# Transposing q, k and x of a whole block with one DMA each, and loading the ninth chunks of two batches together

## The chip, the cores and the metric

The kernel runs on one core of a Trainium2 chip. The metric is the device time of one execution in microseconds. Engines: TensorE (PE, with its weight loads shown as PEld), VectorE (DVE), ScalarE (ACT), GpSimd (POOL) and SyncE (SP). In this kernel SP does no arithmetic: its queue issues, in program order, all loads and all DMA transposes. POOL's queue issues nearly all stores of the output.

## The reference

Attention within chunks of 64 positions (8 batches, 8 heads, 576 positions, so nine chunks per batch and head, head dimension 64), then a feed-forward layer with squared ReLU over the 4608 tokens:

```python
q_c = q.reshape(B, H, nc, 64, D)          # the same for k and v
scores = np.matmul(q_c, k_c.transpose(0, 1, 2, 4, 3)) / np.sqrt(D)
attn = softmax(scores)                    # over the last axis
x = np.matmul(attn, v_c)                  # -> tokens (B*S, H*D)
h = np.maximum(x @ w_in, 0.0)             # 512 -> 2048
out = h * h @ w_out                       # 2048 -> 512
```

Inputs and output are float32; the kernel's matmuls take bf16 operands.

## The kernel before

The tokens are cut into 18 **groups** of 256 (four chunks of one batch), and two groups make a **block** (`blocks`), nine in all, numbered 0 to 8. Eight chunks of a batch fill two groups; the ninth chunks of all batches are collected in groups 14 and 15 (`rest`), which form block 7. `is_whole(g)` is false for these two alone. Within a group `t` (0, 1) is the 128-token tile and `p` the half of 64 partitions in it.

A group passes through these steps, whose names are the keys of the plan further down:
- loads (`qk_pieces`, `v_pieces`): q in one DMA for a whole group, k in two (one per `t`), V in even heads (`v_even`) and odd heads (`v_odd`, whose chunks sit on the opposite half of the partitions). For a group of ninth chunks every chunk has its own DMA: four of q, four of k, eight of V. The list from `runs(g)` says which stretches belong together.
- `C` (`cast_qk`): q and k are cast to bf16 into `qkb`, by POOL for groups below 8 and by ScalarE from there on.
- `TD` (`transpose_qk_dma`): one DMA transpose from `qkb` to `qkT` (16 tiles of 128 by 128), from group 4 on. Earlier groups are transposed by TensorE.
- `SC` (`scores`): 32 small matmuls of `qkT` into PSUM and one exponential on ScalarE into `e`.
- `AV` (`values`): 32 small matmuls of `e` with V, and the division by the sums on VectorE into `x`.
- `XT` (`transpose_x`): x is transposed into the block's `xT`, by one DMA per group from group 6 on (8 tiles).

Then the block goes through the layer: `ffn_in` (16 hidden tiles, four 512-column matmuls each, ReLU on ScalarE, square on VectorE or ScalarE into `gT`), and `ffn_out` (seven products of a Strassen-like scheme with 16 matmuls each; block 0 uses a plain form).

The order is written by hand. The program runs block after block; each yield of `ffn_in` and `ffn_out` is a **slot** (16 of the hidden layer, or 32 in block 1, then 14 of the output). `plan` says which step of another block is put in after which slot: while block j runs its layer, attention of block j+1 (`nxt`) is done (SC, AV, XT), and block j+2 (`far`) is loaded, cast and transposed (C, TD). One load is issued per slot of `go_slots`. For j from 3 on C stands at slots 18 and 22 and TD at 20 and 24; in j = 2 two slots later or so, in j = 1 at 36, 40 and 42, 45. The schedule is manual: each engine executes its instructions in this order[...].

Buffers: `qk` input tiles 5, `qkb` 2, `qkT` 4, `e` 3, `x` 3 groups, `xT` 2 blocks.

Of the kernel before, what the change touches and what calls it, by code (L numbers as in the profile page):

```python
# [10 lines left out]
FP32 = mybir.dt.float32  # L11
BF16 = mybir.dt.bfloat16
# [5 lines left out]
def kernel(  # L18
# [22 lines left out]
    blocks = [[g, g + 1] for g in range(0, n_grp, 2)]  # L41


    CH = GT // 4
    n_ch = S // CH
    whole = [[(b, CH * (4 * i + c)) for c in range(4)] for b in range(B) for i in range(2)]
    rest = [[(b, CH * (n_ch - 1)) for b in range(b0, b0 + 4)] for b0 in range(0, B, 4)]
    chunks = whole[:-2] + rest + whole[-2:]

    def is_whole(g):  # L50
# [27 lines left out]
    NV = 5  # L78
    NO = 2 * NV + 1
    v_even = [w_pool.tile([128, 2, n_hp, D + 1], FP32, name=f"ve_sb{i}") for i in range(NV)]  # L80
    v_odd = [w_pool.tile([128, n_hp, D + 1], FP32, name=f"vo_sb{i}") for i in range(NO)]
    for vt in v_even:
        nc.gpsimd.memset(vt[:, :, :, D:D + 1], 1.0)
    for vt in v_odd:
        nc.gpsimd.memset(vt[:, :, D:D + 1], 1.0)

    qk = {}

    def runs(g):

        for t in range(2):
            (b, s), (b1, s1) = chunks[g][2 * t:2 * t + 2]
            if b == b1:
                yield t, 0, 2 * CH, b, s
            else:
                yield t, 0, CH, b, s
                yield t, CH, CH, b1, s1

    def qk_pieces(g):
        q_sb = in_pool.tile([128, 2, H, D], FP32, name="q_sb")  # L100
        k_sb = in_pool.tile([128, 2, H, D], FP32, name="k_sb")
        qk[g] = (q_sb, k_sb)

        def pairs(dst, src, p, m, b, s):
            return lambda: nc.sync.dma_start(
                out=dst.rearrange("p t h d -> p (t h d)")[p:p + m // 2, :].rearrange(
                    "p (h e) -> p h e", h=H),
                in_=src[b, :, s:s + m, :].rearrange("h (s i) d -> s h (i d)", i=2))

# [8 lines left out]
        for t, p, m, b, s in runs(g):  # L118
            yield lambda t=t, p=p, m=m, b=b, s=s: nc.sync.dma_start(
                out=k_sb[p:p + m, t, :, :],  # L120
                in_=k[b, :, s:s + m, :].rearrange("h s d -> s h d"))

# [4 lines left out]
    for g in range(n_grp):  # L127
        if is_whole(g):
            if g % 2 == 0:
                first = n_odd  # L130
                n_odd += 5
            b, s = chunks[g][0]
            for c in range(4):
                odd_tile[g, c] = first + g % 2 * 2 + (c + 1) // 2
            odd_loads[g] = [(first, CH, CH, b, s), (first + 1, 0, 2 * CH, b, s + CH),
                            (first + 2, 0, 2 * CH, b, s + 3 * CH)] if g % 2 == 0 else [
                                (first + 3, 0, 2 * CH, b, s + CH), (first + 4, 0, CH, b, s + 3 * CH)]
        else:
            for c in range(4):
                odd_tile[g, c] = n_odd + c // 2  # L140
            odd_loads[g] = [(n_odd + c // 2, (1 - c % 2) * CH, CH, b, s)
                            for c, (b, s) in enumerate(chunks[g])]
            n_odd += 2

    def v_pieces(g):
        for t, p, m, b, s in runs(g):
            yield lambda t=t, p=p, m=m, b=b, s=s: nc.sync.dma_start(
                out=v_even[g % NV][p:p + m, t, :, 0:D],
                in_=v[b, 0::2, s:s + m, :].rearrange("h s d -> s h d"))
        for n, p, m, b, s in odd_loads[g]:  # L150
            yield lambda n=n, p=p, m=m, b=b, s=s: nc.sync.dma_start(
                out=v_odd[n % NO][p:p + m, :, 0:D],
                in_=v[b, 1::2, s:s + m, :].rearrange("h s d -> s h d"))

    def go(pieces):
# [55 lines left out]

    def transpose_qk(g, q_pool, k_pool):
        if ("qkT", g) not in state:
            state["qkT", g] = att_pool.tile(
                [128, 2, 2, n_hp, 128], BF16, name="qkT", bufs=4)
        qkT = state["qkT", g]
        for which, pool in enumerate((q_pool, k_pool)):
            if pool is None:
                continue
            copy = nc.scalar.copy if which else nc.vector.tensor_copy  # L220
            if pool is ps_ffn:
                bank = pool.tile([128, 512], FP32, name="ps_ffn")
            else:
                bank = pool.tile([128, 1024], FP32, name="ps_att")
            bank = bank.bitcast(BF16)[:, 0:1024]
            transpose_paired(g, which, bank)
            copy_paired(copy, qkT[:, which], bank)
# [22 lines left out]
                rhs=ident[:, None, :].to_broadcast([128, m, 128]), start=True, stop=True)  # L250

    def cast_qk(g):
        qkb = att_pool.tile([128, 2, 2 * H * D], BF16, name="qkb", bufs=2)
        state["qkb", g] = qkb

        copy = nc.gpsimd.tensor_copy if g < 8 else nc.scalar.copy
        q_sb, k_sb = (x.rearrange("p t h d -> p (t h d)") for x in qk[g])
        copy(
            out=qkb[:, 0].rearrange("p (i h d) -> p i h d", i=2, h=H),
            in_=q_sb.rearrange("p (h i d) -> p i h d", h=H, i=2))  # L260
        copy(out=qkb[:, 1], in_=k_sb)

    def transpose_qk_dma(g):
        qkb = state.pop(("qkb", g))
        qkT = att_pool.tile([128, 2, 2, n_hp, 128], BF16, name="qkT", bufs=4)
        state["qkT", g] = qkT
        nc.sync.dma_start_transpose(
            out=qkT.rearrange("c w t h q -> c (w t h) q"),
            in_=qkb.rearrange("p w c -> p (w c)"))

    def scores(g):
        qkT = state.pop(("qkT", g))
# [10 lines left out]
        for hp in range(n_hp):  # L283
            for t in range(2):
                for a in range(2):
                    for p in range(2):
# [5 lines left out]
                            lhsT=qkT[64 * a:64 * a + 64, 1, t, hp, cols],  # L292
                            rhs=queries(a, t, hp, p),
                            start=True, stop=True)
        e = att_pool.tile([128, 2, n_hp, 2, 64], BF16, name="e")
        state["e", g] = e
        e_out, s_in = e.rearrange("p a h t q -> p (a h t q)"), ps
        if by_plane:
# [4 lines left out]
    def values(g, tiles=(0, 1)):  # L303
        e = state["e", g]
        veb = v_even[g % NV].bitcast(BF16)
        vob = [v_odd[odd_tile[g, c] % NO].bitcast(BF16) for c in range(4)]
        if 0 in tiles:
            state["x", g] = att_pool.tile([128, 2, n_hp, 2, D], BF16, name="x", bufs=3)
# [22 lines left out]
    def transpose_x(g):  # L331
# [16 lines left out]
        copy = nc.vector.tensor_copy if g == blocks[1][0] else nc.scalar.copy  # L348
        copy(out=dst, in_=psb)

    C, TD = cast_qk, transpose_qk_dma
    SC, AV, XT = scores, values, transpose_x

    def TA(g):
# [58 lines left out]
    def ffn_out(j):  # L413
# [50 lines left out]
        def store(dma, o_sb, half, col, t):  # L464
            g = blocks[j][half]
            b, s0 = chunks[g][0]
            t0 = b * S + s0
            if not is_whole(g):

                for p in range(2):  # L470
                    dma.dma_start(
                        out=out.rearrange("(b s) d -> s b d", s=S)[
                            s0:s0 + CH, b + p:b + 4:2, col:col + HD],
                        in_=o_sb[p * CH:(p + 1) * CH].rearrange("p (t d) -> p t d", d=HD))
# [135 lines left out]
    for j, grps in enumerate(blocks):  # L610
# [15 lines left out]
        elif j == 1:  # L626
# [7 lines left out]
                    at(slot, f, g)  # L634
            for i, g in enumerate(far):
                at(36 + 4 * i, C, g)
                at(42 + 3 * i, TD, g)
            at(2, sum_quarters(b11_p_b12, b11, b12), None)
            at(12, sum_quarters(b12_p_b22, b12, b22), None)
            at(20, sum_quarters(b21_p_b22, b21, b22), None)  # L640
            phases = [ffn_in(1, [(0, 256, FT_ORDER), (256, 256, FT_ORDER)]), ffn_out(1)]
        else:
            loads, go_slots = pieces(far), range(32)
            slots = {SC: (6, 6), AV: (9, 13), XT: (12, 16), C: (18, 22), TD: (20, 24)}
            if j == 3:
                slots.update({SC: (8, 8), AV: (10, 14), XT: (13, 17)})
                go_slots = [*range(6), *range(13, 32)]
# [15 lines left out]
        slot = 0  # L663
        for phase in phases:
# [40 lines left out]
```

## Time and profile before

| what | value |
|---|---|
| median of 3 runs | 288.24 us (284.66 to 289.51) |
| profiled execution: time, span | 286.88 us, 285.1 us |
| TensorE busy | 270.0 us (95%) |
| VectorE, ScalarE, POOL busy | 186.4, 163.3, 57.6 us |
| SP's DMA queue (q1) | 137744 packets, 47.33 MB, 76.2% of 16 engines |
| DMA transposes of q,k | 14, median 6.6 us from issue to landing |
| DMA transposes of x | 12, median 3.4 us |
| k loads of 128 KB, V loads of 64 KB (ninth chunks among them) | 8 at 3.9 us; 8 even at 3.5 and 24 odd at 3.9 us |

"Busy" counts the time in which an engine executes; in TensorE's case the ends of pipelined matmuls are modelled. The granted TensorE clock was 1.00 all through. The list of DMA issues gives for each kind the median time from issue to landing, waiting behind other transfers included. Times in the timeline count from the start of the span.

### The profile page before, as it was taken

What the parts mean: (1) busy time and instruction counts of PE and PEld (TensorE: products, weight loads), DVE (VectorE), ACT (ScalarE), POOL (GpSimd) and SP (SyncE); (2) the same over time, 40 slices, a digit from 0 to 9 for tenths busy, and PEclk for the clock granted to TensorE, in tenths of its full rate; (3) what the DMA queues carried; (4) which work ended last, traced back from release to release, by engine and by line L of the source; (5) the groups of instructions that cost most, each with busy time, mean ns of one, the idle gap of its engine ahead of it and who ended that gap; (6) DMA issues with size and microseconds to landing.
All of it is one profiled execution on the core that took longest, in us unless ns stands there. A gap on an engine that the chain in (4) does not pass through costs nothing. (4 is left out here: it accounts for less than half of the span.)

```text
span 285.1 us, 7166 instructions
## 1 busy us (share of the span) xinstructions
PE 270.0 (95%) x2951; PEld 175.5 (62%) x2954; DVE 186.4 (65%) x303; ACT 163.3 (57%) x277; POOL 57.6 (20%) x92
## 2 busy tenths in 40 slices
PE   2999999999999999999999999999799989999994
PEld 1554454788774587458645864586358734874583
DVE  1254614898943695589549954995389538965792
ACT  1557705786358762966396639663866287218710
POOL 2028935153171004000300030003000400050012
PEclk9999999999999999999999999999999999999999
DMA  7999999999999999999999899599999962132003
GB/s 204 236 298 322 380 351 223 328 225 213 213 232 259 229 215 247 261 233 170 256 219 215 176 260 245 107 134 196 212 221 184 257 113 39 37 96 55 1 24 125
DMA packets 140817, 57.10 MB, mean 200 GB/s; under 512 B 110640, under 2 KB 137520, under 8 KB 140784
## 3 DMA queue, kind: packets, MB, share of 16 engines
q1 hardware_dynamic: 137744, 47.33, 76.2%
q0 software_dynamic: 2896, 9.18, 9.7%
q8 instruction: 23, 0.38, 0.6%
q10 hardware_dynamic: 144, 0.13, 0.1%
q14 instruction: 10, 0.08, 0.1%
HBM read 36.70 MB, written 9.44 MB: 162 GB/s over the span
## 5 line engine op out<-in xcount | busy, mean ns | idle before, releaser
L380 PE MATMUL ps_ffn<-xT,w_in_bf 128*128 128x512 bf16 (+1 forms) x648 | 130.5, 356 | 0.9 <-POOL w_in_bf L169 0.3
L395 DVE TENSOR_TENSOR gT<-rl 128x512 bf16<-128x512 f32 (+2 forms) x130 | 73.6, 593 | 65.4 <-ACT rl L391 63.6
L391 ACT ACTIVATE rl<-ps_ffn 128x512 f32<-128x512 f32 (+2 forms) x162 | 86.0, 548 | 27.3 <-PE ps_ffn L380 24.4
L380 PEld LDWEIGHTS <-w_in_bf 128*128 128x128 bf16 x648 | 61.2, 98 | 58.0 <-POOL w_in_bf L169 1.0
L448 PEld LDWEIGHTS <-w_st 128*128 128x128 bf16 x640 | 61.7, 98 | 8.8 <-DVE w_st L408 1.4
L408 DVE TENSOR_TENSOR w_st<-gT 128x2048 bf16<-128x2048 bf16 x40 | 47.3, 1219 | 0.2
L448 PE MATMUL ps_ffn<-w_out_bf,w_st 128*128 128x256 bf16 x384 | 45.1, 273 | 0.3
L476 POOL DMA_DIRECT2D out_dram<-o_sb x25 | 17.8, 714 | 128.3 <-DVE o_sb L408 123.7
L448 PE MATMUL ps_ffn<-w_sum,w_st 128*128 128x256 bf16 x256 | 29.6, 273 | 0.0
L448 PEld LDWEIGHTS <-gT 128*128 128x128 bf16 x256 | 24.7, 98 | 4.6 <-DVE gT L395 0.3
L325 DVE TENSOR_TENSOR x<-ps_att,rec 128x512 bf16<-128x512 f32 x36 | 24.9, 691 | 1.2
L528 ACT COPY o_sb<-ps_ffn 128x512 f32<-128x512 f32 (+1 forms) x8 | 4.5, 560 | 35.4 <-PE ps_ffn L448 35.4
L301 ACT ACTIVATE e<-ps_att 128x1024 bf16<-128x1024 f32 x18 | 18.0, 1021 | 6.7 <-PE ps_att L290 6.7
L393 ACT ACTIVATE gT<-rl 128x512 bf16<-128x512 f32 (+2 forms) x32 | 18.4, 576 | 1.0
L448 PE MATMUL ps_ffn<-w_out_bf,gT 128*128 128x256 bf16 x128 | 15.4, 273 | 0.0
L448 PE MATMUL ps_ffn<-w_sum,gT 128*128 128x256 bf16 x128 | 15.3, 273 | 0.0
L538 PE MATMUL ps_ffn<-w_out_bf,gT 128*128 128x512 bf16 x61 | 14.2, 379 | 0.3 <-issue 0.2
L169 POOL CAST w_in_bf<-w_st 128x512 bf16<-128x512 f32 (+2 forms) x12 | 9.6, 816 | 19.2 <-DMA w_st<-in_moe_w_in_dram 18.9
L290 PEld LDWEIGHTS <-qkT 64*64 64x64 bf16 x576 | 6.2, 110 | 9.4 <-issue 3.6
L501 ACT COPY n<-ps_ffn 128x512 f32<-128x512 f32 (+1 forms) x9 | 4.8, 539 | 11.9 <-PE ps_ffn L448 11.9
L290 PE MATMUL ps_att<-qkT 64*64 64x64 bf16 x576 | 8.3, 198 | 3.4 <-DMA qkT<-qkb 3.0
L317 PEld LDWEIGHTS <-e 64*64 64x64 bf16 x576 | 6.5, 107 | 7.4 <-issue 2.2
(53 smaller groups left out, 167.7 us busy)
## 6 DMA issues: line engine op xcount, KB each, us to landing
q_sb<-in_q_dram SPq DMA_DIRECT2D x16, 512.0 KB, 6.4
out_dram<-o_sb POOLq DMA_DIRECT2D x29, 256.0 KB, 4.6
k_sb<-in_k_dram SPq DMA_DIRECT2D x24, 256.0 KB, 5.9
ve_sb<-in_v_dram SPq DMA_DIRECT2D x32, 128.0 KB, 4.2
w_st<-in_moe_w_in_dram SPq DMA_DIRECT2D x8, 512.0 KB, 6.3
w_st<-in_moe_w_out_dram SPq DMA_DIRECT2D x8, 512.0 KB, 5.8
vo_sb<-in_v_dram SPq DMA_DIRECT2D x24, 128.0 KB, 3.8
k_sb<-in_k_dram SPq DMA_DIRECT2D x4, 512.0 KB, 6.7
```

Of the source, the lines that this page charges most:

```text
L169: copy(out=dst, in_=st[:, rows].rearrange("p a (f t) -> p a t f", t=2)[:, :, t])
L290: nc.tensor.matmul(out=ps[64 * c:64 * c + 64, o0:o0 + 64], lhsT=qkT[64 * a:64 * a + 64, 1, t, hp, cols], rhs=queries(a, t, hp, p), start=T ...
L301: nc.scalar.activation(out=e_out, in_=s_in, func=AF.Exp, scale=scale)
L325: nc.vector.tensor_tensor(out=x[:, t].rearrange("p h a d -> p a h d"), in0=o[:, :, :, 0:D], in1=rec.to_broadcast([128, 2, n_hp, D]), op=AL ...
L380: nc.tensor.matmul(out=h[:, 0:n], lhsT=w_in_bf[:, dt, ft * 128:(ft + 1) * 128], rhs=xT[:, c // 128:(c + n) // 128, dt, :], start=(dt == 0) ...
L391: nc.scalar.activation(out=rl[:, 0:n], in_=h[:, 0:n], func=AF.Relu)
L393: nc.scalar.activation(out=gT[:, ft, c:c + n], in_=rl[:, 0:n], func=AF.Square)
L395: nc.vector.tensor_tensor(out=gT[:, ft, c:c + n], in0=rl[:, 0:n], in1=rl[:, 0:n], op=ALU.mult)
L408: engine.tensor_tensor(out=out, in0=in0, in1=in1, op=op)
L448: nc.tensor.matmul(out=outs[t], lhsT=a[:, i, t * 128:(t + 1) * 128], rhs=b[:, i, :], start=(first and i == 0 and (last or t == 0)), stop=( ...
L476: dma.dma_start(out=out[t0:t0 + HT, col:col + HD].rearrange("(t p) d -> p t d", p=128), in_=o_sb.rearrange("p (t d) -> p t d", d=HD))
L538: nc.tensor.matmul(out=o_ps[tt], lhsT=gT[:, ft, tt * 128:(tt + 1) * 128], rhs=w_out_bf[:, ft, :], start=(ft == 0), stop=(ft == n_ft - 1))
```

## The change

Three edits:
1. From group 6 on, q and k of both groups of a block are cast into one `qkb` tile (one buffer of a block in place of two of a group) and transposed by one DMA of 32 tiles (`TDB`), after both casts. `qkT` becomes a block tile with two buffers. Groups 4 and 5 keep a DMA each. C and TDB stand at slots 18, 20 and 22 (j = 2: 20, 22 and 24; j = 1: 36, 40 and 44).
2. The x of both groups of a block is one tile (two buffers), and one DMA of 16 tiles transposes it at the second group's place in the plan. `e` goes from three buffers to two.
3. The ninth chunks are ordered so that batches b and b+1 are the two tiles `t` of a half of the partitions and b+4, b+5 those of the other. k of a half then comes in one DMA (two per group instead of four), V's even and odd heads in two each (four per group instead of eight). `v_odd` becomes one tile with eleven slices, so that two neighbouring slices can be one destination.

```diff
-    rest = [[(b, CH * (n_ch - 1)) for b in range(b0, b0 + 4)] for b0 in range(0, B, 4)]
+    rest = [[(b0 + t + p * (B // 2), CH * (n_ch - 1)) for t in range(2) for p in range(2)]
+            for b0 in range(0, B // 2, 2)]
...
-    v_odd = [w_pool.tile([128, n_hp, D + 1], FP32, name=f"vo_sb{i}") for i in range(NO)]
+    v_odd = w_pool.tile([128, NO, n_hp, D + 1], FP32, name="vo_sb")
...
+        if not is_whole(g):
+            for p in range(2):
+                b, s = chunks[g][p]
+                yield lambda p=p, b=b, s=s: nc.sync.dma_start(
+                    out=k_sb[p * CH:(p + 1) * CH].rearrange("p t h d -> p (t h) d"),
+                    in_=k.rearrange("b h s d -> s (b h) d")[s:s + CH, b * H:(b + 2) * H])
+            return
...
+        if not is_whole(g):
+            n = odd_tile[g, 0] % NO
+            for a, dst in ((0, v_even[g % NV]), (1, v_odd[:, n:n + 2])):
+                for p in range(2):
+                    b, s = chunks[g][p ^ a]
+                    yield lambda a=a, p=p, b=b, s=s, dst=dst: nc.sync.dma_start(
+                        out=dst[p * CH:(p + 1) * CH].rearrange("p t h d -> p (t h) d")[:, :, 0:D],
+                        in_=v.rearrange("b (h a) s d -> a s (b h) d", a=2)[
+                            a, s:s + CH, b * n_hp:(b + 2) * n_hp])
+            return
...
     def cast_qk(g):
-        qkb = att_pool.tile([128, 2, 2 * H * D], BF16, name="qkb", bufs=2)
-        state["qkb", g] = qkb
+        if g % 2 == 0:
+            state["qkb", g // 2] = att_pool.tile(
+                [128, 2, 2, 2 * H * D], BF16, name="qkb", bufs=1)
+        qkb = state["qkb", g // 2][:, g % 2]
...
+    def transpose_qk_dma_block(g):
+
+        for i in range(2):
+            state["qkT", g + i] = qkT_of(g + i)
+        nc.sync.dma_start_transpose(
+            out=state["qkT", "block", g // 2].rearrange("c g w t h q -> c (g w t h) q"),
+            in_=state["qkb", g // 2].rearrange("p g w c -> p (g w c)"))
...
-        e = att_pool.tile([128, 2, n_hp, 2, 64], BF16, name="e")
+        e = att_pool.tile([128, 2, n_hp, 2, 64], BF16, name="e", bufs=2)
...
         if g >= FIRST_DMA_X:
-            nc.sync.dma_start_transpose(out=dst, in_=x.rearrange("p t h a d -> p (t h a d)"))
+
+            if g % 2:
+                nc.sync.dma_start_transpose(
+                    out=xTs[j].rearrange("p t h q -> p (t h) q"),
+                    in_=state["x", "block", g // 2].rearrange("p g t h a d -> p (g t h a d)"))
             return
...
                 at(36 + 4 * i, C, g)
-                at(42 + 3 * i, TD, g)
+            at(44, TDB, far[0])
...
-            slots = {SC: (6, 6), AV: (9, 13), XT: (12, 16), C: (18, 22), TD: (20, 24)}
+            slots = {SC: (6, 6), AV: (9, 13), XT: (12, 16), C: (18, 20), TD: 22}
...
-                slots = {SC: (8, 10), AV: (12, 15), XT: (15, 18), C: (20, 23), TD: (22, 25)}
+                slots = {SC: (8, 10), AV: (12, 15), XT: (15, 18), C: (20, 22), TD: 24}
...
-            for f in (C, TD):
-                for i, g in enumerate(far):
-                    at(slots[f][i], f, g)
+            for i, g in enumerate(far):
+                at(slots[C][i], C, g)
+            if far:
+                at(slots[TD], TDB, far[0])
```

More of the change, by code (lines that the diff above doesn't have):

```diff
@@ L80 @@
     v_even = [w_pool.tile([128, 2, n_hp, D + 1], FP32, name=f"ve_sb{i}") for i in range(NV)]
-    v_odd = [w_pool.tile([128, n_hp, D + 1], FP32, name=f"vo_sb{i}") for i in range(NO)]
+    v_odd = w_pool.tile([128, NO, n_hp, D + 1], FP32, name="vo_sb")
     for vt in v_even:
         nc.gpsimd.memset(vt[:, :, :, D:D + 1], 1.0)
-    for vt in v_odd:
-        nc.gpsimd.memset(vt[:, :, D:D + 1], 1.0)
+    nc.gpsimd.memset(v_odd[:, :, :, D:D + 1], 1.0)
     qk = {}
[L89 to L97, printed above, removed]
     def qk_pieces(g):
@@ L117, in qk_pieces @@
             return
[L118 to L121, printed above, removed]
+        if not is_whole(g):
[5 more added lines that the diff above has]
+            return
+        for t in range(2):
+            b, s = chunks[g][2 * t]
+            yield lambda t=t, b=b, s=s: nc.sync.dma_start(
+                out=k_sb[:, t, :, :],
+                in_=k[b, :, s:s + 2 * CH, :].rearrange("h s d -> s h d"))
     odd_tile, odd_loads = {}, {}
@@ L138 @@
         else:
+            assert n_odd % NO < NO - 1
             for c in range(4):
                 odd_tile[g, c] = n_odd + c // 2
-            odd_loads[g] = [(n_odd + c // 2, (1 - c % 2) * CH, CH, b, s)
-                            for c, (b, s) in enumerate(chunks[g])]
             n_odd += 2
     def v_pieces(g):
[L146 to L149, printed above, removed]
+        if not is_whole(g):
[8 more added lines that the diff above has]
+            return
+        for t in range(2):
+            b, s = chunks[g][2 * t]
+            yield lambda t=t, b=b, s=s: nc.sync.dma_start(
+                out=v_even[g % NV][:, t, :, 0:D],
+                in_=v[b, 0::2, s:s + 2 * CH, :].rearrange("h s d -> s h d"))
         for n, p, m, b, s in odd_loads[g]:
             yield lambda n=n, p=p, m=m, b=b, s=s: nc.sync.dma_start(
-                out=v_odd[n % NO][p:p + m, :, 0:D],
+                out=v_odd[p:p + m, n % NO, :, 0:D],
                 in_=v[b, 1::2, s:s + m, :].rearrange("h s d -> s h d"))
@@ L213, in transpose_qk @@
         if ("qkT", g) not in state:
-            state["qkT", g] = att_pool.tile(
-                [128, 2, 2, n_hp, 128], BF16, name="qkT", bufs=4)
+            state["qkT", g] = qkT_of(g)
         qkT = state["qkT", g]
@@ L261, in cast_qk, with qkT_of @@
         copy(out=qkb[:, 1], in_=k_sb)
+    def qkT_of(g):
+        if g % 2 == 0:
+            state["qkT", "block", g // 2] = att_pool.tile(
+                [128, 2, 2, 2, n_hp, 128], BF16, name="qkT", bufs=2)
+        return state["qkT", "block", g // 2][:, g % 2]
     def transpose_qk_dma(g):
-        qkb = state.pop(("qkb", g))
-        qkT = att_pool.tile([128, 2, 2, n_hp, 128], BF16, name="qkT", bufs=4)
-        state["qkT", g] = qkT
+        state["qkT", g] = qkT = qkT_of(g)
         nc.sync.dma_start_transpose(
             out=qkT.rearrange("c w t h q -> c (w t h) q"),
-            in_=qkb.rearrange("p w c -> p (w c)"))
+            in_=state["qkb", g // 2][:, g % 2].rearrange("p w c -> p (w c)"))
+    def transpose_qk_dma_block(g):
[4 more added lines that the diff above has]
+            in_=state["qkb", g // 2].rearrange("p g w c -> p (g w c)"))
     def scores(g):
@@ L305, in values @@
         veb = v_even[g % NV].bitcast(BF16)
-        vob = [v_odd[odd_tile[g, c] % NO].bitcast(BF16) for c in range(4)]
+        vob = [v_odd[:, odd_tile[g, c] % NO].bitcast(BF16) for c in range(4)]
         if 0 in tiles:
-            state["x", g] = att_pool.tile([128, 2, n_hp, 2, D], BF16, name="x", bufs=3)
+            if g % 2 == 0:
+                state["x", "block", g // 2] = att_pool.tile(
+                    [128, 2, 2, n_hp, 2, D], BF16, name="x", bufs=2)
+            state["x", g] = state["x", "block", g // 2][:, g % 2]
         x = state["x", g]
@@ L349, in transpose_x @@
         copy(out=dst, in_=psb)
-    C, TD = cast_qk, transpose_qk_dma
+    C, TD, TDB = cast_qk, transpose_qk_dma, transpose_qk_dma_block
     SC, AV, XT = scores, values, transpose_x
@@ L472, in store @@
                         out=out.rearrange("(b s) d -> s b d", s=S)[
-                            s0:s0 + CH, b + p:b + 4:2, col:col + HD],
+                            s0:s0 + CH, b + p * (B // 2):b + p * (B // 2) + 2, col:col + HD],
                         in_=o_sb[p * CH:(p + 1) * CH].rearrange("p (t d) -> p t d", d=HD))
```

## The prediction

> **What bounds the kernel now.** I read the page first: busy time by engine, then the chain that ended last, then the list of waits, then the timeline of TensorE (PE) and of SP's queue around each wait.
>
> ```profile
> PE 270.0 (95%) x2951; PEld 175.5 (62%) x2954; DVE 186.4 (65%) x303; ACT 163.3 (57%) x277; POOL 57.6 (20%) x92
> ...
> PE 17%; DMA 4%; DVE 1%; issue 0%
> ```
> ```profile
> PE ps_att L290 <- DMA qkT<-qkb: 3.0, 3, 1.6
> ...
> PE ps_ffn L380 <- DMA xT<-x: 0.2, 1, 0.2
> ```
> TensorE bounds it: 270.0 of 285.1 us. Of the 15.1 us idle, 6.4 lie in the first 20 us (13.62 busy there) and 3.9 in the last 25 (21.14 busy), which the change doesn't touch. What it can remove is the second fence (waits of PE from 20 us on): three waits for transposed q,k and one for transposed x, **3.2 us** or 1.1%. The timeline puts them in block 5 (0.3 at 146.9), block 7 (1.55 at 203.97) and block 8 (1.17 at 232.66, and x 0.22 at 225.78). A change within 2% (5.8 us) can hardly be told from none.
>
> ```profile
> 160.00:180.00 20.00, 20.00 (x220) 12.71 (x218) 12.60 (x20) 12.65 (x20) 2.85 (x4) 1.00 0.98 222
> 180.00:200.00 20.00, 19.90 (x178) 14.25 (x177) 15.81 (x23) 11.20 (x18) 2.85 (x4) 1.00 0.90 151
> ```
> The last two columns are the DMA engines' share and GB/s. DMA is as full as TensorE up to 220 us, and falls to 151 GB/s just where block 7 (the ninth chunks) is loaded in 64 and 128 KB pieces. SP's queue shows the result: block 8's loads begin at 203.94 only, after block 7's late V pieces, and block 8's transposes are the end of the chain:
> ```profile
> 221.07 4.41 DMA xT<-x
> 225.48 7.13 DMA qkT<-qkb
> ...
> 232.66 0.45 PE ps_att L290 x32
> ```
> The other end is block 3 (groups 6 and 7), where nothing waits today:
> ```profile
> 79.70 7.51 SPq L267 DMA_TRANSPOSE qkT<-qkb  x2
> 87.27 1.79 SPq L147 DMA_DIRECT2D ve_sb<-in_v_dram  x2
> ```
> ```profile
> 83.18 1.04 POOL L261 CAST qkb<-k_sb 128x1024 bf16<-128x1024 f32 x1 [0.57 <-DMA k_sb<-in_k_dram]
> ```
> ```profile
> 90.76 0.45 PE L290 MATMUL ps_att<-qkT 64*64 64x64 bf16 x32
> ...
> 92.97 0.45 PE L290 MATMUL ps_att<-qkT 64*64 64x64 bf16 x32
> ```
> Group 6's transpose is issued at 79.70 and lands 6.6 us later (86.3); group 7's at 84.25, when its cast ends (84.22), and lands at 91.84. The scores need them at 90.76 and 92.97: slack 4.4 and 1.1 us.
>
> [...] block 6's first transpose, before the output stores of POOL's queue, lands in 4.0 us, the second, beside them, in 8.6:
> ```profile
> L267 SPq DMA_TRANSPOSE qkT<-qkb x2: 1765/2765/3765, 162.6 to 164.5; - x2
> DMA to landing us min/median/max: 4.0/6.3/8.6
> ```
> [...]
>
> **The change part by part.** Call T the time from issue to landing of one transpose of a whole block's q,k (1 MB). No row shows it. From below: a 16-tile transpose alone lands in 3.8 us, an 8-tile one (x) in 3.1, so 32 tiles would take 3.8 + 2*0.75 = 5.3[...]. From above: pairs issued back to back took 10.2 (block 8: 222.44 to 232.62), 10.5 (block 6) and, with V loads between, 10.6 and 11.6 (blocks 4 and 5). The same packets pass the same engines beside the same stores, so I take the pair. In block 3 three stores fall into it, not four[...]: **T = 9.6**.
>
> *Block 3 loses.* The one transpose needs both casts, so it is issued at 84.25, and group 6 loses its start of 4.5 us. Landing 84.25 + 9.6 = 93.85, needed at 90.76: **+3.1 us** of TensorE wait, new. Queued behind it on SP: nine V loads and block 4's q,k. SP is free again after the issue, today 3.99 + 2.97 us, so at 91.2 instead of 87.27, 3.9 late. Five V loads at about 0.6 are issued by 94.3 and land 3 later, 97.3; the values matmuls want them at 95.18 + 3.1 = 98.3. Hidden, by 1 us. ScalarE may wait about a microsecond for block 4's last k (105.35 + 3.9), in the output phase where nothing asks for ScalarE.
>
> *Blocks 4 to 6: no loss, little margin.* The scores of both groups stand together there or nearly, so it was the later landing that counted. Block 4: SP reaches the transpose after x (one issue of 2 x 1.27 from 103.54), a V-even load 0.6 and a V-odd load 1.6, with gaps 108.5; allowed are 118.90 - 108.5 = 10.4. Block 5: x's first transpose no longer interrupts (1.3 us), so SP gets there at 134.8 (cast done by 133); allowed 11.3 to 11.4. Block 6: 159.9 + 2.5, so 162.6; allowed 173.03 - 162.6 = 10.4. T = 9.6 to 10.4 fits each: 0, and block 5's 0.3 goes.
>
> *Block 7 gains.* Loads fall from 32 DMAs to 20 (k 8 to 4, V 16 to 8), bytes the same. Today SP stands still from 176.6 to 180.33 for x of group 12 with k loads behind it; afterwards all q,k and half of V are ahead of the single x transpose. x of group 13 is ready at 183.97: 2.5 of issue, four V loads at 0.6, 189. ScalarE's second cast moves from slot 22 to 20, one product of 1.75 us, and ends near 189.6 (today 191.52). 189.6 + T = 199.2 to 200.1, needed at 201.97: **-1.55**.
>
> *Block 8 gains.* Its loads start near 197 instead of 203.94, x transposes are no longer late (-0.22), the cast ends near 219.5; 219.5 + 10.2 = 229.7, needed at 231.05: **-1.17**.
>
> *At nothing:* the moved cast stands before ScalarE's copy of n2, which then ends near 133.6 in block 5; the product that overwrites its bank starts at 133.93. Waiting for both x groups: x lands 2.6 to 8 us ahead of the next hidden layer except in block 8, and the second group's transpose was the later one already. Eleven memsets into one lie under 18 us of waiting for weights. One v_odd tile, and two buffers of e instead of three: the program's waits name the same matmuls as before. Reordered ninth chunks: same stores, same count.
>
> *Sum:* +3.1 - 0.3 - 1.55 - 1.17 - 0.22 = **-0.1 us** on a profiled execution of 286.88 us (span 285.1, 1.8 around it): 286.8. The median of the runs, 288.24, is 1.4 above; I predict **288.1**.
>
> **The rivals.** *(a) One large transpose is cheap*, T at 5 to 6.5[...]. For it: the singles at 3.8 to 4.0. Against: every pair. Block 3 then loses nothing and 3.2 goes: 285.0, still within 2%. *(b) Slower: T is long.* The whole block waits for the last of its 32 tiles, so T beyond the allowed 6.5, 10.4, 11.3, 10.4 and (block 8) 11.3 is wait. At T = 11.8: 5.3 + 1.4 + 0.5 + 1.4 + 0.5 - 3.2 = 5.9, the 2%; from there it decides. At 12.2: 11.1 - 3.2, 296. For it: block 5's 11.6. Against: that pair had a V load and a pause inside. *(c) The change doesn't do what it says.* Excluded: the program's order shows 14 DMA transposes instead of 26, of 32 and 16 tiles, and 12 loads fewer.
>
> **How the numbers follow.** Forecast 0.58 (T 7 to 11.5: -3 to +4), (a) 0.22, (b) 0.17, else 0.03. The range takes (a) with a median that falls 1 us lower, 283.8, and (b) up to T near 12, 294.5. Faster by over 2% needs more than all waits that are there: 0.05, for a favourable draw. Slower 0.17, within 0.78.
>
> **What would show it.** Right: a new wait of about 3 us at L290's successor near 91 us, waits near 204 and 232 gone, block 8's loads starting before 198, block transposes landing 9 to 11 us after issue. Wrong: T below 7 or above 11.8, or V loads late in block 3.

## The result, and the profile after

The changed kernel takes 296.17 us (median of 6 runs, 294.44 to 299.25), the kernel before on the same chip 287.23 (284.66 to 290.97): ratio **1.034**, 95% interval 1.026 to 1.043. It is slower, and the time lies above the predicted range. The profiled execution has a span of 292.8 us, 7.7 more than before. Ratios compare only executions within 1.5% of the fastest of their kernel, medians take all; in five experiments below (e1, e6, e8, e15, e18) the profiled execution was slower than that, so there the waits are read as places rather than as sizes.

The page of the changed kernel: busy time, the slices of TensorE and its granted clock, SP's DMA queue, and the chain that ended last.

```profile
PE 272.3 (93%) x2954; PEld 175.7 (60%) x2954; DVE 186.3 (64%) x303; ACT 162.9 (56%) x277; POOL 55.9 (19%) x82
...
PE   2989999999993699999998999999999999999994
...
PEclk9999999999998599999999999999999999999998
...
q1 hardware_dynamic: 137168, 47.33, 77.9%
...
PE 60%; DVE 14%; DMA 12%; ACT 6%; SPq 4%; issue 3%; POOL 1%; ACTq 0%
```

Two slices near 95 us stand out: TensorE at 3 tenths, and the clock at 8 and 5. TensorE is busy 2.3 us *more* than before for the same matmuls; a few tenths of that are three matmuls missing from the record of before (2951 of 2954), the rest fits the lower clock. The list of TensorE's waits from 20 us on (total, times, longest) and the chain of waits around the place (start, length):

```profile
PE ps_att L313 <- DMA qkT<-qkb: 8.3, 2, 6.9
PE ps_ffn L410 <- DVE xT L379: 0.2, 1, 0.2
PE ps_att L343 <- ACT e L324: 0.2, 1, 0.2
```
```profile
77.69 6.36 DMA k_sb<-in_k_dram
84.10 1.05 POOL qkb L272
85.17 12.30 DMA qkT<-qkb
98.16 3.53 PE ps_ffn L410 x8
...
145.92 10.98 DMA qkT<-qkb
157.66 2.70 PE ps_ffn L410 x12
```

This is block 3, the place that the prediction named, with a wait of 6.88 us where 3.1 were expected: group 7's last k lands, POOL casts it, the transpose of 32 tiles takes 12.30 us, and TensorE stands. The second wait (1.46 us) is block 5's. The waits near 204 and 232 us are gone. TensorE's timeline after the wait (start, length, instruction), and below it the same eight matmuls in the kernel before:

```profile
97.51 0.64 PE L313 MATMUL ps_att<-qkT 64*64 64x64 bf16 x32 [6.88 <-DMA qkT<-qkb]
98.09 3.60 PE L410 MATMUL ps_ffn<-xT,w_in_bf 128*128 128x512 bf16 x8
```
```profile
91.14 1.90 PE L380 MATMUL ps_ffn<-xT,w_in_bf 128*128 128x512 bf16 x8
```

Eight matmuls of 512 columns take 3.60 us, 450 ns each, against 1.90 us before. Stretches of the same kernel (PE busy, PEld, DVE, ACT, POOL, then granted clock, DMA share, GB/s) show why:

```profile
91.00:97.50 6.50, 0.00 (x0) 0.00 (x0) 0.57 (x2) 0.27 (x1) 0.00 (x0) 0.64 1.07 163
97.50:101.70 4.20, 4.19 (x47) 1.64 (x50) 0.43 (x1) 1.62 (x2) 0.00 (x0) 0.50 1.38 216
101.70:104.50 2.80, 2.80 (x47) 1.29 (x50) 0.42 (x1) 2.40 (x4) 0.00 (x0) 0.76 1.24 262
104.50:108.00 3.50, 3.50 (x78) 1.80 (x78) 2.47 (x7) 2.49 (x5) 0.00 (x0) 1.00 1.27 252
```

The clock falls to half during the idle time (1.00 up to 92 us, 0.50 from 93 us on) and comes back at about 103 us, some 5.5 us after work has begun again: 6.88 us of idle time, then 0.50. Two other runs of this case show a lowered clock with waits of 2.15 and 2.56 us as their longest (last section).

The balance is easiest in **phases**, from the first hidden-layer matmul of a block to that of the next (us; the phase of block n contains the attention of block n+1, and that of block 8 runs to the end of the last matmul):

| phase of block | 2 | 3 | 4 | 5 | 6 | 7 | 8 |
|---|---|---|---|---|---|---|---|
| before | 28.14 | 28.12 | 28.59 | 28.08 | 29.95 | 29.16 | 26.20 |
| after | 37.60 | 28.12 | 29.65 | 28.07 | 28.38 | 28.08 | 26.20 |

Block 3's attention costs 9.46 us, of which 6.88 are wait; the other 2.58 are put down to the low clock (e11 tests this). Block 5's costs 1.06. Blocks 7 and 8 give back 1.57 and 1.08. With the 0.2 by which phase 2 begins earlier the sum is +7.7 us, the difference of the spans.

### The profile page after: what moved, and what is told of

Same layout as the page of the kernel before. It is cut to its first block, busy times and chain, and to the rows that moved or that the text cites. A ratio compares the mean times of both kernels' runs of the same rounds, so it can differ in the third digit from the quotient of the medians.

```text
span 292.8 us, 7120 instructions
## 1 busy us (share of the span) xinstructions
PE 272.3 (93%) x2954; PEld 175.7 (60%) x2954; DVE 186.3 (64%) x303; ACT 162.9 (56%) x277; POOL 55.9 (19%) x82
## 3 DMA queue, kind: packets, MB, share of 16 engines
q1 hardware_dynamic: 137168, 47.33, 77.9%
## 4 chain that ended last, share of the span: by engine, by line
PE 60%; DVE 14%; DMA 12%; ACT 6%; SPq 4%; issue 3%; POOL 1%; ACTq 0%
PE ps_ffn L410 27%; PE ps_ffn L478 26%; DMA qkT<-qkb 8%; DVE gT L425 6%; PE ps_ffn L568 5%; DVE x L351 4%; ACT rl L421 3%; DMA k_sb<-in_k_dram 2%; DVE w_st L438 2%; DMA w_st<-in_moe_w_in_dram 2%; ACT e L324 2%; SPq L96 1%; SPq L157 1%; SPq L161 1%; PE ps_att L313 1%
## 5 line engine op out<-in xcount | busy, mean ns | idle before, releaser
L410 PE MATMUL ps_ffn<-xT,w_in_bf 128*128 128x512 bf16 (+1 forms) x648 | 132.4, 360 | 0.7 <-POOL w_in_bf L179 0.5
L269 ACT CAST qkb<-q_sb 128x1024 bf16<-128x1024 f32 x10 | 10.5, 1048 | 0.0
```

Of the source, the lines that this page charges most:

```text
L269: copy(out=qkb[:, 0].rearrange("p (i h d) -> p i h d", i=2, h=H), in_=q_sb.rearrange("p (h i d) -> p i h d", h=H, i=2))
L410: nc.tensor.matmul(out=h[:, 0:n], lhsT=w_in_bf[:, dt, ft * 128:(ft + 1) * 128], rhs=xT[:, c // 128:(c + n) // 128, dt, :], start=(dt == 0) ...
```

## Experiments

All take the kernel before or after and change the lines shown. Theories A and B are those of the first runs: A, the loss is block 3's late transpose and nothing else; B, something in the change makes the transposes land late in other blocks too. The tiles' addresses, called theory C in the expectations, came out of the first four runs; D there is edits 2 and 3 by themselves.

**Which part costs?** e1 gives the changed kernel back its two transposes in block 3; e2 all its two transposes per block (casts and transposes at the slots of before; the joined buffers stay), so that edits 2 and 3 remain; e3 is the kernel before with edit 1 alone; e4 is e1 with both transposes at slot 44.

```diff
e1:
-            at(44, TDB, far[0])
+            for i, g in enumerate(far):
+                at(42 + 3 * i, TD, g)
e2, besides e1's:
-            slots = {SC: (6, 6), AV: (9, 13), XT: (12, 16), C: (18, 20), TD: 22}
+            slots = {SC: (6, 6), AV: (9, 13), XT: (12, 16), C: (18, 22), TD: (20, 24)}
...
e4:
-            at(44, TDB, far[0])
+            for g in far:
+                at(44, TD, g)
```

> The changed kernel, but groups 6 and 7 (block 3) have a transpose each again, at slots 42 and 45; all later blocks keep the one of 32 tiles. Theory A (the loss is block 3's late start, its 6.9 us wait and the half clock after it, 9.5 us together): no wait in block 3, about 286 us, ratio to before 0.99 to 1.00. Theory B (a 32-tile transpose is slow wherever it stands, and block 3's long wait only gave the later blocks slack): waits of 1 us or more come up in blocks 4, 5 and 6, whose allowed times are 10.4, 11.3 and 10.4 us, and it stays at 289 to 292 us, ratio 1.01 to 1.02.

> The changed kernel with edit 1 undone: a q,k transpose per group everywhere, at the slots of the kernel before; x per block and the loads of the ninth chunks two batches at a time stay. Theory A: as the run with only block 3 mended, or 1 us better (block 5's wait goes): 284 to 286 us, ratio 0.985 to 0.995. Theory B: clearly better than that run, by 3 us or more. If the ninth chunks' loads are what gained in blocks 7 and 8, the wait near 204 us of the kernel before is gone here too.

> The kernel before with edit 1 alone (one 32-tile q,k transpose per block from group 6 on, casts at slots 18 and 20); x per group, ninth chunks in single loads. Theory A: block 3 loses 9 to 10 us, blocks 7 and 8 gain nothing or wait more: 296 to 299 us, ratio 1.035 to 1.045. Theory that x or the loads carry the loss: under 290 us, ratio under 1.01.

> The changed kernel, but in block 3 the one transpose of 32 tiles is replaced by two of 16 issued one after the other at its place, slot 44, after both casts. If a large transpose costs what two small ones in a row cost (only its late start and the stores beside it make it long): group 6 lands about 7 us after issue and group 7 about 12, so that scores of group 6 wait 1 to 2 us and those of group 7 about 3: 291 to 294 us. If 32 tiles in one DMA are slow for themselves: the second lands within 10 us and the waits sum to under 3 us: 287 to 290 us.

| run | median us | ratio (interval) | waits for q,k in the profile |
|---|---|---|---|
| e1 | 294.31 | 1.023 (1.011 to 1.034) | 0.29 (block 2), 2.49 (block 3), 0.74 (block 4), 4.39 (block 5) |
| e2 | 292.51 | 1.025 (1.017 to 1.033) | 0.83 (block 3), 0.23 (block 5), 2.81 (block 6), 1.34 (block 7); x 1.54 |
| e3 | 288.93 | 1.013 (1.006 to 1.020) | 2.56 (block 3), 1.01 (block 5) |
| e4 | 294.70 | 1.027 (1.015 to 1.039) | 0.30 (block 2), 0.70 (block 3), 1.64 (block 4), 3.98 (block 5); x 1.10 |

Theory A falls: with two transposes in block 3, as before the change, the kernel is still 2.3% slower. More telling, e2 has all transposes of q,k as before and is slower by 2.5%, while e3, which has all of edit 1, loses only 1.3%. So the larger part of the loss belongs to edits 2 and 3, which had been costed at nothing or as a gain. And e3 shows no wait in blocks 7 and 8: the gain there is edit 1's, without edit 3's loads. e4 did not become what was meant: SP waits for the data and not for the slot, so group 6's transpose was issued at 82.74, before group 7's casts, and group 7's at 86.62. It says nothing about two transposes issued after both casts.

What e1, e2 and e4 share with the changed kernel, and e3 doesn't, is the memory layout. Eleven tiles `v_odd` of 1040 bytes per partition, each rounded up to 1056, became one of 11440, rounded up to 11456: every tile allocated behind it (w_st, q, k, qkT, e, x, xT, qkb, gT, output) starts 160 bytes lower (x by one buffer of e more, a multiple of 256). Before, all these started at multiples of 128 bytes; after, none does.

**Is it the address?** e6 and e7 shift the kernel before by 32 and 64 bytes, with a tile that nothing uses; e5 gives the changed kernel its 160 bytes back, e8 does so with e1. Later e16 and e17 shift by a full 128 relative to the kernel before, once each way, as controls.

```diff
e5, e8 (40 columns; e17: 8):
     nc.gpsimd.memset(v_odd[:, :, :, D:D + 1], 1.0)
+    w_pool.tile([128, 40], FP32, name="pad")
e6 (8 columns; e7: 16, e16: 32):
     for vt in v_odd:
         nc.gpsimd.memset(vt[:, :, D:D + 1], 1.0)
+    w_pool.tile([128, 8], FP32, name="pad")
```

> The changed kernel with one unused tile of 160 bytes per partition behind v_odd. In the kernel before every tile from w_st on (q, k, qkb, qkT, x, xT, o_sb) begins at a multiple of 64 bytes; one v_odd tile in place of eleven, each rounded up, moved all of them by 160 bytes to odd multiples of 32. The pad moves them back; nothing else differs. Theory C (the addresses make the DMAs slower, the transposes above all): block 3's transpose lands about 11 us after issue in place of 12.3, groups 4 and 5 in about 4.2 us as in the kernel with edit 1 alone, and the time falls from 296 to 286 to 290 us, ratio 1.00 to 1.015. Theory D (x per block or the ninth chunks' loads cost it): no change, 294 to 297 us.

> The kernel before with one unused tile of 32 bytes per partition behind v_odd, so that all later tiles begin at odd multiples of 32 bytes; no other edit. Theory C: transposes of q,k take 6 us and more also alone (group 5: 3.8 before), TensorE waits at several blocks, 289 to 293 us, ratio 1.015 to 1.03. Theory D: as the kernel before, 284 to 287 us.

> The kernel before with an unused tile of 64 bytes: the later tiles begin at odd multiples of 64 bytes (before: multiples of 128). If 64 bytes are what counts: 284 to 287 us, ratio within 0.995 to 1.005. If 128 or more: slower, 287 to 292 us.

> The changed kernel with the pad of 160 bytes and with a transpose for each of groups 6 and 7 in block 3 (slots 42 and 45). Theory C: no wait in block 3 nor half clock after it, blocks 7 and 8 keep their gain of about 3 us: 282 to 285 us, ratio 0.99 to 1.00. Theory D: as the run with block 3 mended and no pad, 291 to 295 us.

> A control: the kernel before with 128 bytes of padding, so that every tile that 32 and 64 bytes moved is moved again, but by a full 128. If the start's remainder by 128 is what counts: q1 at 215 to 221 us (about 76% of 285), as before, and a ratio of 0.995 to 1.005. If any shift of these tiles slows the kernel, or if it is the padding and the new build: q1 at 225 us or more and a ratio of 1.02 to 1.04.

> A control: the changed kernel with 32 bytes of padding in place of 160, so that its tiles start at multiples of 128 bytes again, but 128 below those of the kernel before. If the remainder by 128 counts: as with 160 bytes of padding, one wait of 4 to 5 us in block 3, q1 at 220 us or less, span 288 to 290 us, ratio 1.005 to 1.02. If only the very addresses of before are good: as the changed kernel, q1 at 225 us or more, span 292 us or more, ratio 1.025 to 1.04.

In the next table "remainder" is the start of the loads' tiles (w_st, q, k) and of the later ones (xT, qkb, output) modulo 256 bytes, from the program's memory layout; qkT, e and x share the remainder of the loads' tiles. "q1" is SP's DMA queue: its share on the page times the span, that is, the time that the packets of the same 47.33 MB took, per DMA engine. Packets overlap (the stretches above show shares over 1, up to 1.38), so this measures how slow packets are, not how long an engine is occupied.

| kernel | remainder | q1, us | median us | ratio (interval) |
|---|---|---|---|---|
| before | 128, 0 | 217.2 | | 1 |
| after | 224, 96 | 228.1 | 296.17 | 1.034 (1.026 to 1.043) |
| e6 before, +32 | 160, 32 | 228.0 | 299.69 | 1.033 (1.016 to 1.050) |
| e7 before, +64 | 192, 64 | 229.1 | 300.57 | none given; before on that chip: 289.2 |
| e16 before, +128 | 0, 128 | 205.6 | 288.59 | 1.004 (1.001 to 1.007) |
| e5 after, +160 | 128, 0 | 217.0 | 290.40 | 1.011 (1.002 to 1.020) |
| e17 after, +32 | 0, 128 | 207.8 | 289.91 | 1.011 (1.006 to 1.016) |
| e8 after with e1, +160 | 128, 0 | 215.0 | 288.33 | none given; before on that chip: 289.2 |

Thirty-two bytes of padding, and nothing else, make the kernel before as slow as the change did; 160 bytes, or 32 that lead to another multiple of 128, take two thirds of the change's loss away. My guess that multiples of 64 would do (e7) missed. Single transposes show it too. Group 5's stays a transpose of 16 tiles in every version; its row and landing time in the kernel before, and then in e6:

```profile
L267 SPq DMA_TRANSPOSE qkT<-qkb x1: 1593/1593/1593, 66.9 to 66.9; - x1
...
DMA to landing us min/median/max: 3.8/3.8/3.8
```
```profile
L268 SPq DMA_TRANSPOSE qkT<-qkb x1: 2954/2954/2954, 67.3 to 67.3; - x1
...
DMA to landing us min/median/max: 6.2/6.2/6.2
```

It lands 2.4 us later. The pair shown is one of the widest: over all runs this transpose took 3.8 to 4.8 us where every moved tile starts at a multiple of 128 (5.4 in e15) and 4.9 to 6.4 elsewhere. e6's profile has four waits, 11.9 us in all, where the kernel before has three with 3.0:

```profile
PE ps_att L291 <- DMA qkT<-qkb: 11.9, 4, 4.2
```

With its addresses restored (e5) the changed kernel shows the wait that the prediction named and no other for q,k:

```profile
PE ps_att L314 <- DMA qkT<-qkb: 4.8, 1, 4.8
```

One wait, in block 3: issued at 85.43, landed 10.07 us later. Phases 35.12, 28.12, 28.25, 28.08, 28.38, 28.07: +7.0 in block 3, -0.3, -1.57, -1.08 elsewhere, +3.9 in the span. Single profiles differ here: at the same addresses e3's transpose of block 3 was issued at 82.4 and took 11.1 us, and e17's was issued at 81.0 and took 11.6, so what e17 gains in block 3 are earlier loads. e3 and e17 also keep waits of 1.01 and 2.44 us in block 5. e8's two transposes take block 3's wait away (phase 2 28.14), but waits of 1.18 and 2.79 stand in blocks 4 and 5, so the single transpose is tight there as well: theory B is right that far.

**Which tiles?** e12 moves only the tiles behind q and k by 64 bytes (qkT, e, x, xT, qkb, gT, output), e13 moves w_st, q and k by 64 and all later ones by 128.

```diff
e12 and e13:
     att_pool = ctx.enter_context(tc.tile_pool(name="att", bufs=3))
+    pad_pool = ctx.enter_context(tc.tile_pool(name="pad", bufs=1))
...
+    pad_pool.tile([128, 16], FP32, name="pad2")
     qk = {}
e13 besides:
+    w_pool.tile([128, 16], FP32, name="pad")
```

> The kernel before with 64 bytes of padding behind the q,k tiles only: w_st, q and k stay at multiples of 128 bytes, every later tile (qkT, e, x, xT, qkb, gT and the output among them) moves to an odd multiple of 64. If the transposes' tiles are what is slow when moved: group 5's lone transpose takes 4.8 us or more and q1's share of the span is 78% or above, with a time near 294 to 300 us. If the loads' destinations q and k are what is slow: 76% as before, the lone transpose near 4.0, and 284 to 289 us.

> The kernel before with 64 bytes of padding ahead of w_st and 64 more behind the q,k tiles: only w_st, q and k move to odd multiples of 64 bytes, all later tiles are at multiples of 128. If the loads' destinations are what is slow: q1 at 78% or above and 294 to 300 us. If the transposes' tiles are: 76% as before and 284 to 289 us. If both count, each of the two kernels shows a part of the rise.

One run each: 300.6 and 294.69 us (before on that chip 290.13, median of 27, 283.92 to 296.08), q1 at 228.0 and 225.5 us. e12 shows that the tiles behind q and k count: its loads' tiles are where they were, its time lies above all 27, and group 5's transpose took 6.4 us. e13 leaves the share of the loads open: its time lies within the spread of the kernel before, and its xT, qkb and output moved from remainder 0 to 128, a step that alone is worth 8.6 us of q1 between e18, below, and e17.

**Multiples of 128 or of 256?** The table has an order: q1 is 206 and 208 us where the loads' tiles start at multiples of 256 (e16, e17), 217 where they start 128 above one (the kernel before, e5; 215 in e8), and 228 to 229 at the other remainders, some 5 and 10% more. That 256 is what counts was a guess from this order, and no run shows why a start should cost time. e18 moves xT, qkb and the output tiles of e17 to multiples of 256 too:

```diff
-            rec = att_pool.tile([128, 2, n_hp], FP32, name="rec", bufs=4)
+            rec = att_pool.tile([128, 2, n_hp], FP32, name="rec", bufs=8)
```

> The changed kernel with 32 bytes of padding behind v_odd and eight small buffers for the reciprocals in place of four (128 bytes more), so that every tile that a DMA fills or reads, V's apart, starts at a multiple of 256 bytes. [...] If that is what the shift did: q1 at or below the 208 us of the kernel shifted by 128 (72% of 288), likely about 200, block 3's transpose near 10 us, and a ratio of 1.00 to 1.01, no worse than 1.011. If only the remainder by 128 counts: 206 to 209 us of q1 and the ratio of the kernels with padding, about 1.011. If the low share of the kernels shifted by 128 was chance: q1 back at 215 us or more.

```profile
q1 hardware_dynamic: 137168, 47.33, 69.3%
```

q1 is 69.3% of 287.5, 199.2 us, the lowest of all, as expected. The time did better than expected: 286.61 us, ratio **0.985** (0.972 to 0.998). The same change that was 3.4% slower is about 1.5% faster once its tiles start at multiples of 256. But the four runs lie in two pairs, 283.62 and 284.36, and 288.85 and 289.30, and the ratio rests on the first. The profile is of the second: it still has block 3's wait (3.99 us, the transpose 10.7) and none elsewhere for a DMA. How much of it the first pair has, no trace shows.

**Does the half clock cost what it seems?** e11 is e5 with 22 matmuls more, whose results nothing uses, just ahead of block 3's scores, where TensorE would stand idle.

```diff
+            if j == 2:
+                at(slots[SC][0], lambda _: keep_busy(88), None)
             for f in (SC, AV, XT):
```

> The changed kernel with 160 bytes of padding, and 22 more matmuls of 512 columns (about 4.7 us at full clock, of which nothing is used) in front of block 3's first scores, where TensorE stood idle for 4.8 us. If the half clock after the idle time costs what the clock record shows (about 2.1 us), the wait turns into busy time, no slice near 95 us shows a lower clock, phase 2 falls from 35.1 to about 33 us, and the time to about 288 us (ratio about 1.003). If the lower clock does not come from the idle time, it stays and phase 2 keeps 35 us or more, 290.5 us (ratio 1.011).

289.11 us, ratio 1.013 (0.997 to 1.028): too wide to tell 2 us. The profile does tell. The stretches during and after e5's wait (first), and those of e11 from about the same place on (second):

```profile
91.00:95.50 4.50, 0.00 (x0) 0.00 (x0) 0.66 (x2) 0.35 (x1) 0.00 (x0) 0.76 1.21 295
95.50:100.00 4.50, 4.46 (x68) 1.91 (x72) 0.43 (x1) 1.87 (x3) 0.00 (x0) 0.50 1.35 218
```
```profile
91.00:97.00 6.00, 6.00 (x59) 2.80 (x58) 0.85 (x2) 1.45 (x3) 0.00 (x0) 1.00 1.08 232
97.00:108.00 11.00, 11.00 (x159) 6.63 (x157) 7.15 (x16) 8.14 (x13) 0.00 (x0) 1.00 1.05 230
```

With TensorE kept busy the clock stays at 1.00, no wait for q,k is left, and phase 2 falls from 35.12 to 32.89 us. It is 4.75 longer than before the change, the length of the added matmuls. So 2.2 us of e5's 7.0 were the clock.

**Where does the gain in blocks 7 and 8 come from, and what is the best version?** e9 is e5 with two transposes in blocks 3 to 5 (block 3's by e1's edit) and one from block 6 on. e14 does the same to the kernel before, without edits 2 and 3. e15 keeps two transposes everywhere, but for j > 3 has casts at 18, 20 and transposes at 20, 22. e19 is e14 with all DMA tiles but V's at multiples of 256.

```diff
e9, e14, in the loop's tail:
+            if j < 4:
+                slots.update({C: (20, 23), TD: (22, 25)} if j == 2 else {C: (18, 22), TD: (20, 24)})
             for i, g in enumerate(far):
                 at(slots[C][i], C, g)
-            if far:
+                if j < 4:
+                    at(slots[TD][i], TD, g)
+            if far and j > 3:
                 at(slots[TD], TDB, far[0])
e15, on the kernel before:
+            if j > 3:
+                slots.update({C: (18, 20), TD: (20, 22)})
e19, besides e14's:
+    w_pool.tile([128, 32], FP32, name="pad")
...
-            rec = att_pool.tile([128, 2, n_hp], FP32, name="rec", bufs=4)
+            rec = att_pool.tile([128, 2, n_hp], FP32, name="rec", bufs=8)
```

> The changed kernel with 160 bytes of padding behind v_odd (addresses as in the kernel before), two transposes per block in blocks 3, 4 and 5 at the steps of the kernel before, one 32-tile transpose in blocks 6, 7 and 8. If the loss sits only in block 3's late landing (and in block 5's small margin) and the gain in blocks 7 and 8 comes from the single, earlier transpose: phase 2 back at 28.1, phases 6 and 7 at 28.4 and 28.1 us, span about 282.5, time 282 to 285 us, ratio 0.985 to 0.995. If the ninth chunks' loads slow the transposes of blocks 4 and 5 by themselves, as with two transposes in block 3 alone: waits of 1 to 3 us there, time 286 to 290 us, ratio 1.00 to 1.01.

> The kernel before (its loads, its many v_odd tiles, its addresses), with a single 32-tile transpose per block in blocks 6, 7 and 8 only; blocks 3, 4 and 5 keep their two. If the gain in blocks 7 and 8 belongs to the single transpose with its earlier second cast: phases 6 and 7 at 28.4 and 28.1 us in place of 29.95 and 29.16, nothing lost in phases 2 to 5, span 282 to 283 us, ratio 0.985 to 0.995. If the gain needs the ninth chunks' loads as well: phases 6 and 7 as before, 285 us, ratio 1.00.

> The kernel before with its two transposes per block, but in blocks 6, 7 and 8 the second cast runs two steps earlier (20 in place of 22) and the transposes stand at steps 20 and 22. If what gains in blocks 7 and 8 is the earlier cast and issue: no wait in phases 6 and 7, or under 0.4 us, span 282 to 283 us, ratio 0.985 to 0.995. If it is that one transfer replaces two: waits of 1 us and more stay there, ratio 0.998 to 1.01.

> The kernel before with a single 32-tile transpose from block 6 on, two per block before that, and all its DMA tiles but V's at multiples of 256 bytes. TensorE has no wait left at the addresses of before, so easier transfers can win nothing in the profile: span 281.5 to 282.5 us, q1 near 200 us, ratio 0.99 to 0.997, with less spread between runs. If a wait comes back, or the ratio is 1.00 or more, the single transpose's gain was a matter of chance in its profile.

| run | median us | ratio (interval) | waits for q,k in the profile |
|---|---|---|---|
| e9 | 285.51 | 0.998 (0.994 to 1.002) | 0.56 (block 3), 1.01 (block 5), 0.91 (block 6) |
| e14 | 284.94 | 0.995 (0.991 to 0.998) | none |
| e15 | 286.48 | 0.996 (0.991 to 1.001) | 0.17 (block 5), 2.15 (block 6), 0.87 (block 8) |
| e19 | 283.00 | **0.981** (0.974 to 0.987) | 0.80 (block 4), 1.35 (block 5) |

e14's list of waits has no transpose left (TensorE, from 20 us on):

```profile
PE ps_ffn L393 <- DVE xT L362: 0.2, 1, 0.2
PE ps_ffn L393 <- ACT rl L404: 0.2, 1, 0.2
PE ps_att L330 <- ACT e L314: 0.2, 1, 0.2
```

Phases 6 and 7 are 28.39 and 28.07 us with the loads of before: edit 3 isn't needed for the gain. e15 has no wait in block 7 either, with two transposes, so there the earlier cast looks enough, though in that profile TensorE had waited 2.15 us in block 6 just before; in block 8 a wait of 0.87 stays where one transfer leaves none. How much of block 8's gain needs the single transfer rests on one profile, and the ratios of e14 and e15 (0.995 and 0.996) don't tell the two apart. e19 beats both kernels, though not through the waits of its profile, which it has and e14 has not: its runs lie between 282.24 and 285.17 us, those of before beside it between 285.67 and 296.79. q1 is 72.2% of 283.4, 204.6 us. But e14 and e19 ran on different chips, and their fastest runs are only 0.6 us apart (282.82 and 282.24): that the addresses add to e14's gain rests on the two ratios, and no profile shows at which wait.

## Why the prediction was wrong

- **The failed step is the term "One v_odd tile", listed under "At nothing".** The prediction looked only at which matmuls the waits name. The tile moves the start of every later one by 160 bytes: the packets of SP's queue take 228 us instead of 217, and of the 3.4% only 1.1 are left with the addresses restored (e5) or 128 bytes from there (e17). A shift of 32 bytes in the kernel before costs 3.3% by itself (e6), and the changed kernel with two transposes in every block (e2) still loses 2.5%.
- **"T = 9.6" was too small**: block 3's transpose took 12.30 us, and 10.1 to 11.6 in the five profiles with every moved tile at a multiple of 128 (e3, e5, e11, e17, e18). So the addresses are one part of the miss. The other is the choice of the shortest pair, 10.2 us, out of pairs of 10.2 to 11.6, less 0.6 for a store, an estimate of mine that no run shows. The block's 3.1 us became 6.88: 2.70 from T, 0.92 because the issue came at 85.17 instead of 84.25 (the last k landed later), 0.1 from an earlier need.
- **The half clock is missing from the sum**: 2.58 us after a wait of 6.88, and e11 shows 2.2 of this kind in e5. A wait was priced at its own length.
- **"Blocks 4 to 6: no loss, little margin"** held for blocks 4 and 6, not for 5: T was 10.98, within the allowed 11.3, but the issue came at 145.92, 1.7 us later than the 134.8 of the prediction once moved by the 9.46 us lost before. In e5 that wait is absent, in e3 and e17 it isn't: the margin is as small as was said. Block 4 held by luck: T was 11.2, over the allowed 10.4, but the issue came 2 us before the 108.5 of the prediction, moved likewise.
- **"Block 7 gains -1.55" and "Block 8 gains -1.17"** came true in size: -1.57 and -1.08 in the phases (x's 0.22 doesn't show beside them). The reason given, fewer and larger loads, was wrong: e3 and e14 gain as much with the old loads, e2 keeps 1.34 us of wait in block 7 with the new ones. In block 7 the cast two slots earlier, which the prediction mentioned beside it, is enough in e15's one profile; in block 8 the single transfer seems to count too.
- **Block 3 as the place of the loss, and rival (b)**, were right: a T beyond 11.8 was named as the point from which the change is slower. It was reached by one block, and the low clock did the rest. That (b) gives 296 us for T = 12.2, close to the 296.17 measured, is chance: its sum has late transposes in blocks 4 to 8 too, where T was 11.2, 11.0, 8.5, 10.8 and 7.9. Rival (a) is out: no 32-tile transpose of the changed kernel landed in less than 7.9 us, where it had 5 to 6.5. Rival (c) is out too. V loads late in block 3 were not seen.
- **The other items "at nothing"**: no wait for x stands in the changed kernel. e2 and e4 show one of 1.5 and 1.1 us in block 4, but e7 and e12, with a transpose of x per group at shifted addresses, have such waits of 1.0 and 1.1 us as well; what the joint one costs is not shown.

## What to carry to other kernels

When an edit changes a tile's shape, compare the start addresses of all tiles behind it before weighing anything else; here starts at multiples of 256 bytes were worth about 5% between the worst and the best version of the same change (1.034 against 0.985, the latter with an interval of 0.972 to 0.998). Price a wait of TensorE of several microseconds at more than its length: here the lower clock added 2.2 and 2.6 us to waits of 4.8 and 6.9. Leave two transfers apart where the first half is needed first (block 3: phase 2 is 28.14 us with two in e8, 35.12 with one in e5); where both are needed at once and late (blocks 7 and 8) merging them did no harm (e14's phases 6 and 7 are 28.39 and 28.07 us against 29.95 and 29.16), and most of what it gained there may be the earlier cast.

## What the hardware did unexpectedly

- The packets of the same 47.33 MB took 199 and 205 us per DMA engine with all moved tiles at multiples of 256 (e18, e19), 206 and 208 with xT, qkb and output at remainder 128 (e16, e17), 212 to 220 with the loads' tiles at 128 instead (the kernel before and all runs at its addresses), and 225 to 231 where some tiles start off multiples of 128. Loads' remainders of 160 to 224 differ by less than 1% (228.0, 229.1, 228.1). No run separates reads from writes.
- Less DMA time isn't less waiting by itself: e16 has 12 us less of q1 than the kernel before and a ratio of 1.004, with waits of 1.32 and 3.69 us in blocks 7 and 8.
- The mean clock of the execution was 0.994 in e15, whose longest wait was 2.15 us, and 0.991 in e3, whose longest was 2.56, but 1.000 in e2, whose longest was 2.48: the length of the longest wait alone doesn't decide. After e3's 2.56 us eight matmuls of 512 columns took 2.96 us instead of 1.90, and the next 32 small ones 0.64 instead of 0.45; the extra time was 1.6 us in all.
- Issuing a 32-tile transpose held SP's queue for 6.83 us in block 3 of the changed kernel, over half of the 12.30 us until it landed.
